# A transformer block on one core: the planner's order replaced by a fixed list, weights split into more tiles, other early loads

## The chip, the cores and the metric

One core of one Trainium2 chip runs the whole kernel. The metric is the device time in microseconds (us) of one execution; lower is better. The core's engines work from queues of their own: PE (TensorE, matmuls; its weight loads are shown as PEld), DVE (VectorE), ACT (ScalarE), POOL (GpSimd) and SP (SyncE, which here issues all transfers but one). They wait for one another by semaphores only.

## What is computed

One transformer block over 2048 rows of 512 columns, in bf16: conditioned layernorm, attention over eight earlier positions in steps of two, and a gated feed-forward layer.

```python
mod = (silu(c) @ w_mod).reshape(1, 6, 1, 512)
sa, ca, ga, sb, cb, gb = mod[:, 0], mod[:, 1], mod[:, 2], mod[:, 3], mod[:, 4], mod[:, 5]
h = layernorm(x) * (1 + ca) + sa
x = x + ga * A(h, wqkv, wo)
h = layernorm(x) * (1 + cb) + sb
x = x + gb * ((gelu(h @ w_gate) * (h @ w_up)) @ w_down)
...
# A: 32 heads of 16; q, k, v = h @ wqkv; position s sees s, s-2, ... s-14
logits = einsum('bhsd,bhswd->bhsw', q, kg) * 16 ** -0.5
o = einsum('bhsw,bhswd->bhsd', softmax(logits), vg)
return o.reshape(B, S, D) @ wo
```

## The kernel before

**Tiling.** The rows are split into five groups of 256, 256, 512, 512 and 512 (`GROUPS`, line 198); group 0 is the first. Everything but x is held with the columns on the partitions. For each group the kernel emits these steps:
- `ln` (line 419): statistics on DVE (L442, L444), the inverse root on POOL (L448), the normed rows xn on DVE (L452), their transpose (on PE, L476, for the first norm of groups 0 to 2 and the second of group 0; otherwise by a transposing DMA, L459), and the scaling by the modulation (ACT L490 or L464, for group 0 also DVE L485), which gives hT or, for the second norm, h2T.
- `emit_qkv` (line 498): the projections (L527), 12 tiles of a PSUM bank for a group of 512 rows, 6 for one of 256, each of 16 or 8 matmuls, copied out by ACT (L532) to qT, kT and vT. vT goes to DRAM (`scr`, L537) and comes back as four shifted loads (`vR`, L541).
- `emit_attention` (line 551): products of q and shifted k on DVE (`pq`, 1.16 us each in a row), folded over the head's 16 columns by PE (L585), a softmax (maxima on DVE L607 to L611, their subtraction on PE L616, exponentials on ACT L623, sums on PE L635, reciprocals on DVE L639, their broadcast on PE L647), products with v (`pv`), folded by PE (L678), the output projection (L693), and the residual sum on DVE (L697); then the second norm.
- `emit_ffn` (line 703): 14 blocks of 128 gate and up columns (L716; two blocks to a tile for 256 rows), gelu on ACT, the product on DVE, and the down matmuls (L738) in chunks of four, four, four and two; then the residual sum (`ot`, L745) and the store.
The gates ga and gb are multiplied into wo (`woP`, L760) and w_down (`WdP`, L763, seven pieces) by DVE.

**What orders the work.** Nothing is issued where it is written. `pe`, `act`, `dve`, `gp` and `dma` append an operation with a cost, its operands, and a priority to a list; `Plan.order` (line 88) then simulates the engines and always takes the operation that can start soonest, by priority among equals. Its transfers cost bytes over a bandwidth (360 GB/s unless given), one behind the other on a queue, and land 2.0 us later. `emit` (line 152) issues the operations in that order, and each engine, and SP with its transfers, runs its part of it strictly in order. The tile framework adds the semaphores, by the tiles and ranges of tiles that instructions touch.

**Loads.** SP first issues x's rows 0 to 255, two blocks of w_mod (512 columns each, for sa and ca), the three parts of wqkv (v, q, k) into one tile, then the rest of the first 1024 rows of x and the other early weights (lines 337 to 351). `late_loads` (line 353) holds gate, up, down and the later x back until group 0's vR has been issued. Warm-up matmuls (L366) run from 1.3 to 6.0 us, and `keep_warm` (L373) repeats two of them at two places, to have PE busy ahead of the first projection.

Of the kernel before, what the change touches and what calls it, by code (L numbers as in the profile page):

```python
# [15 lines left out]
NEG = -1.0e9  # L16

# [22 lines left out]
class Plan:  # L40
# [3 lines left out]
    AHEAD = 3.0  # L44
    MARGIN = {"pe": 0.3, "act": -0.2, "dve": -0.2, "pool": 0.0, "sp": 0.0}
# [42 lines left out]
    def order(self):  # L88
        for o in self.ops:
            for p in o.pre | o.after:  # L90
                p.post.append(o)
        n_pre = {o: len(o.pre | o.after) for o in self.ops}
        ready = [o for o in self.ops if not n_pre[o]]
        engines, pipe, table = {}, {}, None
        placed, made = [], {t: [] for t in self.tags}
        seen = set()

        def start(o):
            at = max([p.end - (p.lat if p.eng == o.eng and not p.dma else 0.0) for p in o.pre], default=0.0)
            for t in o.tiles:  # L100
                if t.tag is not None and t not in seen:
                    before = self.seqs[t.seq][t.at - 1] if t.at else None
                    if before is not None and before not in seen and before not in o.tiles:
                        return None
                    got, bufs = made[t.tag], self.tags[t.tag][1]
                    if len(got) >= bufs:
                        if got[-bufs].left:
                            return None
                        at = max(at, got[-bufs].free)
            return at  # L110

        while ready:
            best = None
            for o in ready:
                at = start(o)
                if at is None:
                    continue
                free = engines.get(o.eng, 0.8)
                if o.dma:
                    at = max(at, pipe.get(o.eng, 0.0) - self.AHEAD)  # L120
                key = (max(free, at + self.MARGIN[o.eng]), o.pri)
                if best is None or key < best[0]:
                    best = (key, o, max(free, at))
            if best is None:
                raise RuntimeError("no operation can be placed: " + str([(o.eng, o.pri) for o in ready]))
            _, o, at = best
            ready.remove(o)
# [35 lines left out]
class Engines:  # L163
    def __init__(self, nc, pl):
        op = pl.op
# [4 lines left out]
        self.dma = lambda n, fn, bw=360e3, **kw: op("sp", 0.55, fn, dma=n / bw, **kw)  # L170
# [3 lines left out]
def kernel(  # L174
# [31 lines left out]
    for tag, bufs in (("xs", 4), ("wqkv", 1), ("woP", 1), ("Wg", 1), ("Wu", 1), ("WdP", 1), ("st", 3), ("mv", 4),  # L206
# [25 lines left out]
    PRI_QKV = (-60, 30, 50, 130, 1050)  # L232

# [27 lines left out]
    def consts_pool():  # L261

# [5 lines left out]

        nc.gpsimd.memset(BC[:], 0.0)
# [9 lines left out]

# [12 lines left out]
    gp(5.0, consts_pool, r=[ident], w=[M, F1, NB, BC, MA, MB], pri=-900)  # L292
# [3 lines left out]
    wqkv = T("wqkv", [P, DT, 3 * D], BF16, "wqkv")  # L296
    woP = T("woP", [P, 4, D], BF16, "woP")
    Wg = T("Wg", [P, DT, F], BF16, "Wg")
    Wu = T("Wu", [P, DT, F], BF16, "Wu")
    WdP = T("WdP", [P, FT, D], BF16, "WdP")  # L300
    wm = [T({2: "oT"}.get(b, "h2T"), [P, 4, D], BF16, "wm") for b in range(6)]
# [14 lines left out]
    def load_x(lo, hi, p, after=()):  # L316
        dma(131e3 * (hi - lo), lambda: nc.sync.dma_start(
# [4 lines left out]
    def load_wm(b, p, after=()):  # L322
        dma(524e3, lambda: nc.sync.dma_start(
# [3 lines left out]
    def load_wqkv(b, p):  # L327
        dma(524e3, lambda: nc.sync.dma_start(
            out=wqkv[:, :, b * D:(b + 1) * D],
            in_=A_wqkv[:, b * D:(b + 1) * D].rearrange("(dt p) n -> p dt n", p=P)), w=[(wqkv, b)], pri=p)  # L330

    act(0.1, lambda: nc.scalar.dma_start(out=crow[:], in_=c), w=[crow], pri=-1000, lat=3.0)
    def load_w(t, src, p, after):
        dma(1835e3, lambda: nc.sync.dma_start(out=t[:], in_=src.rearrange("(dt p) f -> p dt f", p=P)), w=[t], pri=p,
            after=after)

    load_x(0, 2, -1000)
    load_wm(0, -999)
    load_wm(1, -998)
    for i, b in enumerate((2, 0, 1)):  # L340
        load_wqkv(b, -997 + i)
    load_x(2, 4, -990)
    load_x(4, 8, -989)
    load_wm(2, -988)
    for d4 in range(4):
        dma(131e3, lambda d4=d4: nc.sync.dma_start(
# [5 lines left out]

    def late_loads(after):
        load_w(Wg, B_w_gate, -894, after)
        load_w(Wu, B_w_up, -893, after)
        load_x(8, 12, -892, after)
        load_wm(5, -891, after)
        load_w(WdP, B_w_down, -890, after)
        load_x(12, 16, -889, after)
# [24 lines left out]
    pe(0.3, c_cols, r=[crow, one1], w=[c_ps], pri=-990)  # L384
    act(0.2, lambda: nc.scalar.activation(out=scT[:], in_=c_ps[:], func=ACT.Silu), r=[c_ps], w=[scT], pri=-990,
# [3 lines left out]
    def mod_cols(b, b2, p, off):  # L389
        mps = T("psF", [P, 8], F32, "modT_ps")  # L390

        def cols(bb, half):
            for ch in range(4):
                col = half * 4 + ch
                for kt in range(4):
                    nc.tensor.matmul(mps[:, col:col + 1], lhsT=wm[bb][:, kt, ch * P:(ch + 1) * P],
                                     rhs=scT[:, kt:kt + 1], start=(kt == 0), stop=(kt == 3))

        pe(0.42, lambda: cols(b, 0), r=[wm[b], scT], w=[(mps, 0)], pri=p)
        if off == 0:  # L400
            keep_warm(2, (mps, 0), p)
        pe(0.42, lambda: cols(b2, 1), r=[wm[b2], scT], w=[(mps, 1)], pri=p)
# [16 lines left out]
    def ln(g, dst, off, p, seq, tags=("psF", "psF"), sums=None):  # L419
# [49 lines left out]
        for dtp in range(2):  # L469
# [10 lines left out]
            if p == -960 and dtp == 1:  # L480
                keep_warm(2, tp, p)
            for dd in range(2):
                dt = 2 * dtp + dd
                if p == -960 and dd == 1:
                    dve(0.35, lambda dt=dt, dd=dd, tp=tp: nc.vector.tensor_scalar(  # L485
                        out=dst[:, 0:n // P, dt, :], in0=tp[:, dd, 0:n].rearrange("p (c s) -> p c s", s=P), scalar1=scl[:, off // 2 + dt:off // 2 + dt + 1],
# [4 lines left out]
                    out=dst[:, 0:n // P, dt, :], in_=tp[:, dd, 0:n].rearrange("p (c s) -> p c s", s=P), func=ACT.Identity,  # L491
# [307 lines left out]
```

## Time and profile before

| | |
|---|---|
| time, median of 3 runs | 260.44 us (259.02 to 260.95) |
| span of the profiled execution, first to last instruction | 260.6 us |
| PE busy | 242.4 us (93%) |
| DVE busy | 165.3 us (63%) |
| ACT busy | 156.6 us (60%) |
| moved by DMA | 28.84 MB |

The profile is of one execution, and its span is its own time to within what the runs differ by. Busy times of PE are modelled from a pipeline: a matmul is shown with 0.38 us (512 columns) and in a row one starts every 0.216, so the spacing counts and not the mean. The granted clock of PE is given as a share of full speed: 1.00 is 2.4 GHz, 0.50 is 1.2 GHz. "Idle before" in brackets is the time an engine stood still ahead of an instruction, with what ended it.

### The profile page before, as it was taken

What the parts mean: (1) busy time and instruction counts of PE and PEld (TensorE: products, weight loads), DVE (VectorE), ACT (ScalarE), POOL (GpSimd) and SP (SyncE); (2) the same over time, 40 slices, a digit from 0 to 9 for tenths busy, and PEclk for the clock granted to TensorE, in tenths of its full rate; (3) what the DMA queues carried; (4) which work ended last, traced back from release to release, by engine and by line L of the source; (5) the groups of instructions that cost most, each with busy time, mean ns of one, the idle gap of its engine ahead of it and who ended that gap; (6) DMA issues with size and microseconds to landing.
All of it is one profiled execution on the core that took longest, in us unless ns stands there. A gap on an engine that the chain in (4) does not pass through costs nothing.

```text
span 260.6 us, 4271 instructions
## 1 busy us (share of the span) xinstructions
PE 242.4 (93%) x1617; PEld 126.8 (49%) x1632; DVE 165.3 (63%) x313; ACT 156.6 (60%) x278; POOL 21.9 (8%) x43
## 2 busy tenths in 40 slices
PE   7399979979996999999999999999999999999993
PEld 2277735448742477446544444344344444444441
DVE  3277578899999479986289988349946222222111
ACT  2127767676666789748967748943758730666400
POOL 8010200210022000002000005000002000000000
PEclk9869979979999999999999999999999999999999
DMA  6997999999902566405912502210002201100011
GB/s 203 353 252 192 273 399 351 282 233 207 149 3 40 121 160 167 88 3 144 185 43 58 105 3 40 40 43 20 21 0 44 40 0 43 40 0 0 0 43 40
DMA packets 36550, 28.84 MB, mean 111 GB/s; under 512 B 12849, under 2 KB 34610, under 8 KB 36530
## 3 DMA queue, kind: packets, MB, share of 16 engines
q1 hardware_dynamic: 36528, 28.56, 44.6%
q8 instruction: 13, 0.21, 0.4%
q14 instruction: 7, 0.06, 0.1%
q10 hardware_dynamic: 2, 0.00, 0.0%
HBM read 21.40 MB, written 4.28 MB: 99 GB/s over the span
## 4 chain that ended last, share of the span: by engine, by line
PE 83%; DVE 6%; DMA 4%; ACT 3%; issue 1%; POOL 1%; SPq 1%; DVEq 0%; POOLq 0%; ACTq 0%
PE u_ps L716 19%; PE g_ps L716 19%; PE y_ps L738 17%; PE qkv_ps L527 16%; PE x_ps L693 5%; DMA wqkv<-in_A_wqkv_dram 4%; PE o_ps L678 3%; PE LT L585 2%; DVE pq L569 2%; POOL rstd L448 1%; ACT hT L490 1%; DVE st L442 1%; DVE xn L452 1%; PE LT L616 1%; PE rB L647 1%
## 5 line engine op out<-in xcount | busy, mean ns | idle before, releaser
L716 PE MATMUL u_ps<-h2T,Wu 128*128 128x512 bf16 (+1 forms) x280 | 58.5, 341 | 0.0
L716 PE MATMUL g_ps<-h2T,Wg 128*128 128x512 bf16 (+1 forms) x280 | 58.4, 340 | 0.0
L738 PE MATMUL y_ps<-WdP,hht 128*128 128x512 bf16 x216 | 50.3, 379 | 3.0 <-DVE WdP L763 2.5
L527 PE MATMUL qkv_ps<-hT,wqkv 128*128 128x512 bf16 (+1 forms) x240 | 48.7, 358 | 3.7 <-DMA wqkv<-in_A_wqkv_dram 3.2
L725 ACT ACTIVATE gl<-g_ps 128x512 bf16<-128x512 f32 x56 | 33.6, 599 | 29.3 <-PE g_ps L716 29.1
L727 ACT CAST ub<-u_ps 128x512 bf16<-128x512 f32 x56 | 32.8, 586 | 19.8 <-PE u_ps L716 19.8
L728 DVE TENSOR_TENSOR hht<-gl,ub 128x512 bf16<-128x512 bf16 x56 | 23.6, 423 | 32.1 <-ACT ub L727 31.7
L716 PEld LDWEIGHTS <-Wg 128*128 128x128 bf16 x280 | 27.3, 99 | 22.8 <-issue 1.7
L716 PEld LDWEIGHTS <-Wu 128*128 128x128 bf16 x280 | 27.3, 99 | 22.4 <-issue 1.3
L527 PEld LDWEIGHTS <-wqkv 128*128 128x128 bf16 x240 | 27.2, 118 | 22.7 <-issue 8.7
L738 PEld LDWEIGHTS <-hht 128*128 128x128 bf16 x224 | 21.3, 98 | 29.1 <-issue 4.6
L448 POOL TENSOR_TENSOR rstd<-rstd,neghalf 128x2 f32<-128x2 f32 x16 | 16.9, 1077 | 177.0 <-DVE xsum L431 102.5
L569 DVE TENSOR_TENSOR pq<-qT,kT 128x2048 bf16<-128x2048 bf16 x24 | 28.6, 1218 | 0.0
L662 DVE TENSOR_TENSOR pv<-e,vR 128x2048 bf16<-128x2048 bf16 x24 | 28.4, 1219 | 0.0
L745 DVE TENSOR_TENSOR ot<-y_ps,x_sg 128x512 bf16<-128x512 f32 x16 | 10.5, 685 | 23.1 <-PE y_ps L738 23.1
L693 PE MATMUL x_ps<-woP,oT 128*128 128x512 bf16 x59 | 14.9, 379 | 0.3
L434 ACT ACTIVATE xn<-x_sg,xsum 128x512 bf16<-128x512 bf16 x16 | 11.4, 714 | 4.8 <-DVE xsum L431 4.8
L532 ACT CAST kT<-qkv_ps 128x512 bf16<-128x512 f32 x16 | 9.4, 588 | 7.7 <-PE qkv_ps L527 6.5
L532 ACT CAST qT<-qkv_ps 128x512 bf16<-128x512 f32 x16 | 9.4, 586 | 7.3 <-PE qkv_ps L527 7.3
L442 DVE BATCH_NORM_STATS2 st<-x_sg 128x6 f32<-128x512 bf16 x16 | 10.2, 682 | 5.3 <-DMA x_sg<-in_A_x_dram 5.3
L532 ACT CAST vT<-qkv_ps 128x512 bf16<-128x512 f32 x16 | 9.2, 588 | 7.1 <-PE qkv_ps L527 6.7
L697 DVE SCALAR_TENSOR_TENSOR x_sg<-x_ps,x_sg 128x512 bf16<-128x512 f32 x16 | 10.8, 688 | 3.3 <-PE x_ps L693 3.3
(86 smaller groups left out, 189.5 us busy)
## 6 DMA issues: line engine op xcount, KB each, us to landing
vR<-scr SPq DMA_DIRECT2D x24, 260.0 KB, 5.5
wm<-in_w_mod_dram SPq DMA_DIRECT2D x6, 512.0 KB, 7.1
vR<-scr SPq DMA_DIRECT2D x8, 264.0 KB, 5.7
out_dram<-ot SPq DMA_DIRECT2D x16, 128.0 KB, 1.7
Wg<-in_B_w_gate_dram SPq DMA_DIRECT2D x1, 1792.0 KB, 11.2
Wu<-in_B_w_up_dram SPq DMA_DIRECT2D x1, 1792.0 KB, 15.1
WdP<-in_B_w_down_dram SPq DMA_DIRECT2D x1, 1792.0 KB, 12.9
scr<-vT SPq DMA_DIRECT2D x6, 264.0 KB, 2.6
```

The lines of the kernel that those rows point to most:

```text
L442: dve(0.62, lambda i=i, st=st, c0=c0: nc.vector.bn_stats(out=st[:, i, :], in_=x[g, c0 + i]), r=[x.key(g, c0 + i)], w=[(st, i)], pri=p)
L448: gp(0.7, lambda rstd=rstd: nc.gpsimd.tensor_tensor(out=rstd[:], in0=rstd[:], in1=neghalf[:, 0:2], op=ALU.pow), r=[rstd, neghalf], w=[rstd ...
L527: nc.tensor.matmul(ps[:, j - j0, :], lhsT=wqkv[:, dt, b * D + j:(b + 1) * D:4], rhs=hT[g][:, 0:n // P, dt, :], start=(dt == 0), stop=(dt = ...
L532: act(0.49, lambda t=t, off=off, j0=j0, ps=ps: nc.scalar.copy(out=t[:, j0:j0 + nj, off:off + n], in_=ps[:]), r=[ps], w=[(t, j) for j in ra ...
L569: dve(1.16, lambda j=j, wg=wg, t=pq[m]: nc.vector.tensor_tensor(out=t[:], in0=_ap(q[g][:, j, 0:n], [[0, 4], [1, n]]), in1=_ap(k[g][:, j, : ...
L662: dve(1.16, lambda jj=jj, jl=jl, wg=wg, t=pv[m]: nc.vector.tensor_tensor(out=t[:], in0=_ap(e[:, wg, :], [[0, 4], [1, n]]), in1=vR[g][jj][: ...
L693: nc.tensor.matmul(x1_ps[:], lhsT=oT[:, j, c4 * P:(c4 + 1) * P], rhs=woP[:, j, :], start=(j == 0), stop=(j == 3))
L716: nc.tensor.matmul(ps[:, ft - f0, :], lhsT=Wt[:, dt, ft * P:(ft + 1) * P], rhs=h2[g][:, 0:n // P, dt, :], start=(dt == 0), stop=(dt == DT ...
L725: act(0.5, lambda gl=gl, ps=gu[0]: nc.scalar.activation(out=gl[:], in_=ps[:], func=ACT.Gelu_apprx_tanh), r=[gu[0]], w=[gl], pri=p, table=" ...
L727: act(0.49, lambda ub=ub, ps=gu[1]: nc.scalar.copy(out=ub[:], in_=ps[:]), r=[gu[1]], w=[ub], pri=p)
L728: dve(0.37, lambda gl=gl, ub=ub, ht=ht: nc.vector.tensor_tensor(out=ht[:], in0=gl[:], in1=ub[:], op=ALU.mult), r=[gl, ub], w=[ht], pri=p)
L738: nc.tensor.matmul(y_ps[:], lhsT=hh[ft // nf][:, ft % nf, c4 * P:(c4 + 1) * P], rhs=WdP[:, ft, :], start=(ft == 0), stop=(ft == FT - 1))
```

## The change

**The order.** `Plan.order` no longer chooses. A list `ORDER` of 951 operation numbers (in the order in which the program appends them) gives the order; `order` only walks it and computes each operation's planned start `at`, with all transfers on one pipe and a ninth transfer waiting for the landing of the one eight before it. The list puts the parts of a group freely: tiles of one projection or gate and up blocks come in any sequence, and those of different groups are mixed. Decoded, PE's order begins: warm-up, column matmuls of c, fill, modulation 0 and 1, group 0's transposes and fills, group 1's transposes, group 0's projections (q, q, k, v, v, k), group 2's transposes and group 1's projections mixed, group 0's first fold and mask, and from there 12 tiles of group 2's and 10 of group 3's projections between the steps of the first two softmaxes, group 0's and 1's folds and modulation 5, 2, 3, 4, until the first gate tile of group 0 (G0). Group 4's projections stand among group 0's gate and up. At the end PE has three output tiles of group 4 mixed and then all 14 matmuls of the fourth. DVE takes group 3's statistics after group 0's four pq, group 4's in part ahead of group 0's reciprocal, and five of WdP's scalings ahead of group 3's maxima. SP's order begins:

```
x 0-255, x 256-511, x 512-1023, wm01, wq, wkv, woP[3], x 1024-1535, woP[2], woP[1],
x 1536-2047, wm5, scr(0), wm2, vR(0) three pieces, transpose of group 3 (first half), vR(0) fourth piece,
wm3, transpose of group 3 (second half), woP[0], scr(1), Wu[1], vR(1) one piece, Wg[1], wm4, vR(1) two pieces,
scr(2), vR(1) fourth piece, Wg[0], Wu[0], transpose of group 4, ...
```

**Tiles and loads.** wqkv becomes two tiles, wq and wkv (one load each); Wg and Wu become two halves each of 896 columns; the first two blocks of w_mod come as one load wm01 of 1024 columns, into the buffer that WdP takes later; WdP is loaded in two halves. `late_loads` is gone: only the list holds these loads back.

**Layout.** hT and h2T of the groups transposed on PE are `[P, DT, SG]`, so that each of the four column blocks is contiguous; before, all were `[P, 4, DT, P]`.

**Fills.** `keep_warm` becomes `fill`: an operation of planned cost 0.02 whose number of matmuls is set after ordering from the planned gap to PE's next operation. There are four, and group 0's first projection is kept behind them all. The constants of POOL become three operations instead of one.

```diff
+ORDER = [
+    0, 6, 39, 40, 41, 28, 9, 131, 132, 1, 4, 133, 134, 135, 42, 43, 11, 7, 5, 29, 30, 31, 3, 253, 33, 35, 38, 254, 44,
...
+]
...
+        placed = [self.ops[i] for i in ORDER]
...
+            if o.dma and len(landed) >= self.LANES:
+                at = max(at, landed[-self.LANES])
...
+                pipe = max(pipe, at + us) + o.dma
+                o.end = pipe + 2.0 + o.late
...
     def emit(self):
         placed = self.order()
+        pes = [o for o in placed if o.eng == "pe"]
+        for o, q in zip(pes, pes[1:]):
+            if hasattr(o, "fill"):
+                o.fill = max(0, int((q.at - o.at - 0.25) / 0.216))
...
-    wqkv = T("wqkv", [P, DT, 3 * D], BF16, "wqkv")
+    wq = T("wqkv", [P, DT, D], BF16, "wq")
+    wkv = T("wkv", [P, DT, 2 * D], BF16, "wkv")
...
+    Wg = [T("Wg", [P, DT, F // 2], BF16, "Wg") for _ in range(2)]
+    Wu = [T("Wu", [P, DT, F // 2], BF16, "Wu") for _ in range(2)]
+    wm01 = T("WdP", [P, 4, 2 * D], BF16, "wm01")
...
+    def load_cols(t, src, lo, hi, p, bw=380e3):
+        dma(1024.0 * (hi - lo), lambda dq: dq.dma_start(
+            out=t[:], in_=src[:, lo:hi].rearrange("(t p) n -> p t n", p=P)), w=[t], pri=p, bw=bw)
...
     load_x(0, 2, -1000)
-    load_wm(0, -999)
-    load_wm(1, -998)
-    for i, b in enumerate((2, 0, 1)):
-        load_wqkv(b, -997 + i)
-    load_x(2, 4, -990)
+    load_cols(wm01, w_mod, 0, 2 * D, -999)
+    load_cols(wq, A_wqkv, 0, D, -998)
+    load_x(2, 4, -997)
+    load_cols(wkv, A_wqkv, D, 3 * D, -996)
...
-    def late_loads(after):
-        load_w(Wg, B_w_gate, -894, after)
...
+    for i in range(2):
+        load_cols(Wg[i], B_w_gate, i * F // 2, (i + 1) * F // 2, -894 + 2 * i)
+        load_cols(Wu[i], B_w_up, i * F // 2, (i + 1) * F // 2, -893 + 2 * i)
...
-    def keep_warm(n, after, p):
+    fills = []
+
+    def fill(after):
         def run():
-            for i in range(n):
+            for i in range(o.fill):
                 nc.tensor.matmul(wps[:], lhsT=warm[:, 0:P], rhs=warm[:], start=True, stop=True)
...
+        o = pe(0.02, run, r=[warm, after], w=[wps], pri=-960)
+        o.fill = 0
+        fills.append(o)
...
-                        out=dst[:, 0:n // P, dt, :], in0=tp[:, dd, 0:n].rearrange("p (c s) -> p c s", s=P), scalar1=scl[:, off // 2 + dt:off // 2 + dt + 1],
+                        out=dst[:, dt, 0:n], in0=tp[:, dd, 0:n], scalar1=scl[:, off // 2 + dt:off // 2 + dt + 1],
```

## Rows read from the trace of the kernel before

**Rows 1.** The page: busy time of the engines, and the granted clock in 40 slices
```profile
PE 242.4 (93%) x1617; PEld 126.8 (49%) x1632; DVE 165.3 (63%) x313; ACT 156.6 (60%) x278; POOL 21.9 (8%) x43
...
PEclk9869979979999999999999999999999999999999
```

**Rows 2.** Windows by stage: length, busy us of each engine (instructions), PEclk, DMA share, GB/s
```profile
13.50:94.00 80.50, 72.96 (x626) 46.32 (x631) 65.17 (x133) 53.37 (x96) 8.68 (x9) 0.93 0.84 204
...
94.00:256.20 162.20, 161.68 (x934) 77.03 (x941) 94.97 (x166) 100.55 (x177) 7.57 (x6) 1.00 0.23 52
```

**Rows 3.** The chain that ended last, in order of time: start us, us, what
```profile
3.47 9.93 DMA wqkv<-in_A_wqkv_dram
...
13.53 7.61 PE qkv_ps L527 x48
...
21.75 1.84 ACT hT L490 x4
...
26.96 0.99 PE LT L585 x32
...
34.95 7.73 PE qkv_ps L527 x28
...
60.88 0.87 PE g_ps L716 x8
...
132.92 0.86 PE g_ps L716 x4
```

**Rows 4.** Windows over PE's gaps and the slow stretches, columns as in rows 2
```profile
10.40:13.50 3.10, 0.00 (x0) 0.00 (x0) 0.41 (x1) 0.84 (x2) 0.00 (x0) 0.63 1.09 347
...
17.00:18.00 1.00, 1.00 (x7) 0.67 (x6) 1.00 (x3) 0.58 (x1) 0.00 (x0) 0.50 1.08 232
...
32.00:34.80 2.80, 0.82 (x19) 0.62 (x18) 0.98 (x3) 2.79 (x5) 0.00 (x0) 1.00 1.03 401
...
53.00:55.10 2.10, 0.32 (x2) 0.09 (x1) 2.00 (x9) 1.84 (x4) 0.03 (x1) 1.00 1.10 270
...
57.00:58.00 1.00, 1.00 (x6) 0.73 (x5) 0.97 (x3) 0.74 (x2) 0.00 (x0) 0.50 1.10 225
...
81.40:83.90 2.50, 0.01 (x2) 0.03 (x1) 2.50 (x11) 2.50 (x6) 0.59 (x1) 1.00 0.00 0
```

**Rows 5.** Timeline, first and last scaling of group 0's input: start us, us, what
```profile
9.78 0.41 DVE L485 TENSOR_SCALAR hT<-tp,scl,modT 128x256 bf16<-128x256 bf16 x1 [2.02 <-ACT scl L403]
...
11.28 0.41 DVE L485 TENSOR_SCALAR hT<-tp,scl,modT 128x256 bf16<-128x256 bf16 x1 [1.09 <-ACT hT L490]
```

**Rows 6.** The wqkv loads' issue and landing times, and two PE steps of the modulation
```profile
2.37 1.85 SPq L328 DMA_DIRECT2D wqkv<-in_A_wqkv_dram  x3
...
DMA to landing us min/median/max: 8.0/9.0/9.9
...
5.92 0.25 PE L382 MATMUL c_ps<-one,crow 1*128 1x1 bf16 x4
...
8.92 0.55 PE L396 MATMUL modT_ps<-scT,wm 128*128 128x1 bf16 x16 [0.55 <-DMA wm<-in_w_mod_dram]
```

**Rows 7.** Windows: rates of the transfers, in the last column
```profile
0.00:5.00 5.00, 3.74 (x11) 1.42 (x12) 1.53 (x5) 1.28 (x1) 3.92 (x21) 1.00 0.55 179
...
5.00:10.00 5.00, 3.34 (x52) 2.04 (x51) 1.77 (x8) 0.41 (x3) 1.70 (x8) 1.00 1.01 334
...
10.00:15.00 5.00, 1.82 (x10) 1.04 (x9) 1.43 (x4) 1.02 (x2) 0.00 (x0) 0.62 1.11 340
...
50.00:60.00 10.00, 7.77 (x87) 4.89 (x85) 9.65 (x29) 7.29 (x15) 2.54 (x3) 0.83 1.15 221
```

**Rows 8.** Window from the first attention product to group 0's second norm
```profile
20.90:52.50 31.60, 28.54 (x286) 17.66 (x285) 25.23 (x52) 21.64 (x41) 4.01 (x5) 0.95 1.04 300
```

**Rows 9.** The page, DMA issues: KB each, median us to landing
```profile
vR<-scr SPq DMA_DIRECT2D x24, 260.0 KB, 5.5
```

**Rows 10.** Timeline, the last two output additions
```profile
256.13 1.29 DVE L745 TENSOR_TENSOR ot<-y_ps,x_sg 128x512 bf16<-128x512 f32 x2 [4.75 <-PE y_ps L738]
```

More of the change, by code (lines that the diff above doesn't have):

```diff
@@ L40 @@
 class Plan:
[L44 to L45 removed]
+    LANES = 8
     def __init__(self, tc):
@@ L88, in order @@
     def order(self):
[L89 to L99, printed above, removed]
+        engines, pipe, table, landed = {}, 0.0, None, []
+        made, seen = {t: [] for t in self.tags}, set()
+        placed = [self.ops[i] for i in ORDER]
+        assert sorted(ORDER) == list(range(len(self.ops)))
+        for o in placed:
+            at = engines.get(o.eng, 0.8)
+            for p in o.pre:
+                at = max(at, p.end - (p.lat if p.eng == o.eng and not p.dma else 0.0))
             for t in o.tiles:
                 if t.tag is not None and t not in seen:
-                    before = self.seqs[t.seq][t.at - 1] if t.at else None
-                    if before is not None and before not in seen and before not in o.tiles:
-                        return None
+                    seen.add(t)
                     got, bufs = made[t.tag], self.tags[t.tag][1]
                     if len(got) >= bufs:
-                        if got[-bufs].left:
-                            return None
+                        assert not got[-bufs].left
                         at = max(at, got[-bufs].free)
[L110 to L127, printed above, removed]
+                    got.append(t)
             us = o.us
@@ L204, in pool @@
         pl.tag(tag, ctx.enter_context(tc.tile_pool(name=tag, bufs=bufs, **kw)), bufs)
-    for tag, bufs in (("xs", 4), ("wqkv", 1), ("woP", 1), ("Wg", 1), ("Wu", 1), ("WdP", 1), ("st", 3), ("mv", 4),
+    for tag, bufs in (("xs", 4), ("wqkv", 1), ("wkv", 1), ("woP", 1), ("Wg", 2), ("Wu", 2), ("WdP", 1), ("st", 3), ("mv", 4),
                       ("rstd", 4), ("xsum", 4), ("xn1", 2), ("xn2", 2), ("hT", 2), ("qT", 2), ("kT", 2), ("vT", 2), ("vR", 3), ("prod", 6),
@@ L392, in cols @@
         def cols(bb, half):
+            src, at = (wm01, bb * D) if bb < 2 else (wm[bb], 0)
             for ch in range(4):
@@ L518, in emit_qkv @@
         if g == 0:
-            order = [(b, j) for b in (2, 0, 1) for j in range(0, 4, nj)]
+            order = [(b, j) for b in range(3) for j in range(0, 4, nj)]
         for step, (b, j0) in enumerate(order):
@@ L526, in mm @@
                     for dt in range(DT):
-                        nc.tensor.matmul(ps[:, j - j0, :], lhsT=wqkv[:, dt, b * D + j:(b + 1) * D:4],
-                                         rhs=hT[g][:, 0:n // P, dt, :], start=(dt == 0), stop=(dt == DT - 1))
-            pe(0.866, mm, r=[(wqkv, b), hT[g]], w=[ps], pri=p)
+                        nc.tensor.matmul(ps[:, j - j0, :], lhsT=(wkv[:, dt, (b - 1) * D + j:b * D:4] if b else wq[:, dt, j:D:4]), rhs=h_cols(hT, g, dt), start=(dt == 0), stop=(dt == DT - 1))
+            pe(0.866, mm, r=[wkv if b else wq, hT[g]], w=[ps], pri=p,
+               after=fills if g == 0 and step == 0 else ())
             t, off = (q, k, v)[b][g], (0, HALO, HALO)[b]
@@ L536, in emit_qkv @@
             scr = T("scr", [P, njv, row], BF16, "scr")
-            dma(P * njv * row * 2, lambda i=i, scr=scr: nc.sync.dma_start(
+            dma(P * njv * row * 2, lambda dq, i=i, scr=scr: dq.dma_start(
                 out=scr[:], in_=v[g][:, njv * i:njv * (i + 1), 0:row]),
```

104 lines of the change are left out of this document (49 added, 55 removed), and 40 rows, old and new, of the table ORDER.

## The prediction

> **What bounds the kernel now.** I read the page first: TensorE (PE) is busy 93% of the 260.6 us span, and in the slices of 6.5 us its granted clock falls below 0.9 only in slices 2, 3, 6 and 9 [rows 1]. The windows by stage say where the other 7% lies. From 94.0 to 256.2 us PE is busy 161.7 of 162.2 us at full clock. From 13.5 us, where the first projection (the q, k, v matmuls) begins, to 94 it is busy 73.0 of 80.5 us at a mean clock of 0.93 [rows 2]. So an order of the work can win nothing behind 94 us and some 13 us before it.
>
> Then I listed what PE loses between 13.5 and 94 us, from the chain of work that ended last and from windows laid over the gaps [rows 3, 4].
> - Half clock at the start: 48 projection matmuls of 256 columns take 7.61 us. Eight of that size take 0.87 us at full clock, so 48 should take 5.2: 2.4 lost. The granted clock was still 0.50 at 17 to 18 us; from 10.4 to 13.5 PE had stood empty.
> - 32.0 to 34.8 us: busy 0.82 of 2.80, in the first softmax: 2.0 lost. Then half clock again: 28 records of 512 columns take 7.73 us, where 28 x 0.216 (0.86 for four) is 6.05: 1.7 lost.
> - 53.0 to 55.1: busy 0.32 of 2.10, the second softmax and the norm before the first gate matmul: 1.8 lost, and half clock behind it (0.50 at 57 to 58).
> - 81.4 to 83.9: 2.5 lost, DVE busy without a break.
> All idle time is 80.5 - 73.0 = 7.5; less 2.0, 1.8 and 2.5 it leaves 1.2 of small waits, among them group 1's projections, which wait for four scaled inputs one after the other (ACT hT, 1.84 us). The mean clock of 0.93 means 5.6 us; less 2.4 and 1.7 it leaves 1.5 for the third dip. Sum 7.5 + 5.6 = 13.1. At the tail two output additions run one behind the other after the last matmul, 1.29 us [rows 10].
>
> **The change part by part.** *Early loads.* Before the first projection stand, now, 0.26 MB of x, 1.05 of w_mod and 1.57 of wqkv. The three wqkv pieces are issued from 2.37 to 4.2 us and land 8.0, 9.0 and 9.9 us later, the first at 10.4 and the last at 13.4; PE starts at 13.5, after the last, though its first tile needs only the v piece, issued first [rows 3, 6]. Three loads in one tile make that wait, and tiles of their own end it. But the new queue sends x's first 1.05 MB ahead of w_mod. By the rates [rows 7] 0.90 MB had moved by 5 us and 2.57 by 10. The second w_mod block (1.31 MB down the queue) let PE go on at 8.92 [rows 6], when 2.2 MB had moved, and the last wqkv piece (2.88 MB) came when 3.7 had: a load lands when 0.86 MB more than the bytes up to it have moved. So wm01 (2.10 MB) lands at 2.96 MB: 11.2 us at 340 GB/s, 10.2 at the 401 GB/s of the wide weight loads [rows 4]. I take 11.0, near the early rows since x and wq keep narrow rows: the modulation is whole 2 us later than now. wq (2.62 MB) comes at 12.4 (11.5 to 12.7), wkv (3.67) at 15.3 (14.1 to 15.8). Behind wm01 stand two groups of 16 matmuls (1.1), two small copies (0.3) and the four scalings of hT, now in single file between DVE and ACT from 9.78 to 11.69 [rows 5]; with each column block contiguous I take 1.2, two beside two (1.0 to 1.9). First projection: 13.6 us (12.5 to 14.5). No gain: the freed wait is eaten by the later w_mod. The first k tile has to wait for wkv only if both q tiles are done by 15.3; at half clock (1.7 us each) they are not.
>
> *Fill matmuls.* They cost nothing where they fit, as PE has no other work there; one too many delays the next step by 0.2 us. Their number is the planned gap over 0.216. The first gap, behind the column matmuls of c that end at 6.2 [rows 6], reaches to wm01. The plan's own terms (bytes over 360 or 380 GB/s, plus 2.0) set that at 9.0, hence about 9 fills, to 8.1 us. By the rows wm01 is at 11.0: PE empty for 2.9 us. Gaps of 3.1, 2.0 and 1.8 us were followed by half clock, one of 2.5 was not [rows 4]. I keep the first loss of 2.4 us.
>
> *Order of the middle.* Projections of groups 2 and 3 now stand inside the first two softmaxes. Before the first gate matmul PE has 96 x 0.109 + 88 x 0.216 of projections (29.5), three folds of 0.99 [rows 3], 16 matmuls of 512 columns for output projection and modulation (3.5), and 4.7 of transposes, one-column matmuls and softmax steps as the timeline has them: 40.7 us. From 13.6, with 2.4 for the clock, that ends at 56.7. DVE must be ready by then. Its first product needs two q tiles and a k tile, 18.6 at half clock, and a cast of 0.6: 19.2 (17.0 at full clock). From there to the input of group 0's second norm the trace has 25.2 us of DVE work [rows 8]; the new order puts in group 4's statistics (3.1), group 3's norms (1.5), the second softmax's maxima (0.9) and one norm more (0.4), and takes out group 2's (2.1): 29. That is 48.2, with 2 us of waits 50.2, the norm with POOL's root 1.9, transposes and four scalings on ACT 3: 55.1. PE comes 1.6 us later, so the gaps of 2.0, 1.8 and 1.2 go, with the half clock behind them (3.2). The gap of 2.5 goes too: five of WdP's seven scalings stand ahead of group 3's maxima, the other two right behind, and the first down matmul after those. What is late next is the softmax itself: at the first output fold, the second maxima and the second sums PE arrives 0.5 to 1 us before DVE or ACT by this count, and so again in group 2. I take 4 us for all of them (0 to 8; nearest are the two old softmax gaps, 3.8).
>
> *SP queue.* A transfer that waits holds up all behind it. Group 3's two transposing DMAs stand ahead of vR0's last piece and of woP's last quarter, and wait for norms that DVE makes at about 28 and 34 us. Behind them are 5.9 MB (scr and vR of group 1, the gate and up halves), issued from about 35. Stretches full of vR move 221 GB/s [rows 7], and a piece takes 5.5 us to land [rows 9]. 1.05 MB of vR at 200, a little below that, and 4.87 at 375, between the 347 and 401 of rows 4, take 18.2 us, the landing 2.4 (0.86 MB at some 350): the second half needed, Wu0, lands at 55.6 and is wanted at 57.6. Cost nothing; the cover is 2 us. vR0's last piece lands at 35.3 where DVE wants it at 34.5: 0.8, inside the 4.
>
> *Tail.* The last 14 matmuls belong to one output tile: one addition behind them, 0.6 us less.
>
> Sum: gone 7.5 idle, 1.7 and 1.5 of half clock, 0.6 of tail = 11.3; come 4.0 of waits and 0.1 of start; kept 2.4 of half clock. 260.6 - 11.3 + 4.1 = 253.4. The profiled span is 0.2 above the median of the three runs: 253, rounded.
>
> **Rivals.** *The fills hold the clock.* If wm01 lands at the 10.2 of the wide rate, PE never stands empty for more than 2.1 us; then the 2.4 go as well, and 0.8 of the start: 249.8. For it: 401 GB/s in the wide loads [rows 4]. Against it: 334 to 340 GB/s in these very microseconds [rows 7]. The Trainium skill ("DMA: Bandwidth & Descriptors", section "Measured (HBM→SBUF, 128 partitions, SWDGE, issued from GpSimd)") asks for transfers of 1 MiB and more, for three quarters of the peak; it measured another queue than SP's, and wm01 and wkv become such transfers here. By its 425 GB/s for very large ones wm01 would, as an estimate, land a little before 10. No row of this trace reaches that rate in the first 15 us.
>
> *Moved, not removed.* DVE is the bound of the first 70 us: it was busy 25.2 of 31.6 us with all its waits [rows 8], and 2.0 of 2.1 and 2.5 of 2.5 in two of PE's gaps [rows 4]. If each hand-over costs more than I count, PE waits 8 us instead of 4 and falls to half clock once more (1.7): 258.8, no change that can be told. Against it: the chain has PE work beside each softmax step.
>
> *The weights come late (slower).* Place: the gate and up halves at the end of the SP queue's first part, behind transposes and vR. If those 5.9 MB move at vR's 200 GB/s and not at the mixture's 325, they need 29.6 us, Wu0 lands at 67 and PE stands from 57.6 on: 9.4, and half clock behind it 1.7: 264.1. It decides slower from a landing at 66 us on, and takes half of the gain from 61. Against it: 401 GB/s while Wg and Wu move now [rows 4], with vR just ahead of them.
>
> **How the numbers follow.** The forecast 0.64 (249 to 257), the held clock 0.14, moved 0.15, late weights 0.07. A measurement of this kernel can tell about 1%, 2.6 us, from no change. Faster by more: the first two, 0.78. Within: 0.15. Slower: 0.07. Low end of the range: no loss of clock and half the waits, 247.5 with the early start; high end the second rival, 259.
>
> **What would show it.** Right: the first projection at 13 to 14 us and half clock behind it to about 18; then PE without half clock, its waits 4 us in all up to 94, and the first gate matmul at 55 to 58. Wrong: an empty PE of more than 2 us behind 20 us; a gate or up matmul that waits for a DMA; a first projection before 12.5, or at full clock.

## The result, and the profile after

The changed kernel takes 253.05 us (median of 4, 250.94 to 259.33; the highest ran at a lower clock and is left out of the ratio, and without it the median is 252.75); the kernel before, in the runs beside it, 260.69 (259.02 to 261.98). The ratio is 0.967 [0.960, 0.975]: faster. The profiled execution has a span of 250.5 us.

The page of the changed kernel, as [rows 1]: busy time by engine, and the granted clock in 40 slices.

```profile
PE 240.7 (96%) x1637; PEld 126.4 (50%) x1637; DVE 165.9 (66%) x313; ACT 153.4 (61%) x278; POOL 17.9 (7%) x43
...
PEclk9859999999999999999999999999999999999999
```

PE is busy for about as long as before (240.7 us, before 242.4). Of the four slices with a low clock only the second and the third (6.3 to 18.8 us) are left. The windows by stage, as [rows 2]: start and end, length, then busy us of PE, PEld, DVE, ACT, POOL, then PE's clock, DMA share and GB/s.

```profile
13.50:94.00 80.50, 77.94 (x701) 49.88 (x700) 71.85 (x131) 65.21 (x120) 6.12 (x10) 0.97 0.90 216
...
20.00:94.00 74.00, 71.89 (x663) 44.94 (x662) 67.23 (x119) 61.38 (x112) 4.64 (x6) 1.00 0.89 211
...
94.00:247.00 153.00, 153.00 (x864) 71.27 (x861) 86.18 (x160) 85.09 (x153) 5.24 (x6) 1.00 0.21 49
```

From 13.5 to 94 us PE is busy 77.9 us where it was 73.0, and the clock is 0.97 where it was 0.93. Behind 20 us there is no half clock left (1.00), and PE stands still for 2.1 us (74.00 - 71.89). DVE and ACT do more of their work here (71.9 and 65.2 us, before 65.2 and 53.4): 35 attention products on DVE where there were 24, and 47 copies of projections on ACT where there were 35. That work ran behind 94 us before. Behind 94 us PE was almost without a gap before (161.7 of 162.2 us, [rows 2]) and is without one now.

The start, in PE's timeline (start us, us, what; in brackets the idle time before it and what ended it):

```profile
5.94 2.12 PE L403 MATMUL warm_ps<-warm 128*128 128x512 bf16 x9
...
10.59 0.99 PE L429 MATMUL modT_ps<-scT,wm 128*128 128x1 bf16 x32 [2.53 <-DMA wm<-in_w_mod_dram]
...
13.10 0.42 PE L562 MATMUL qkv_ps<-hT,wq 128*128 128x256 bf16 x1
...
13.97 3.36 PE L562 MATMUL qkv_ps<-hT,wq 128*128 128x256 bf16 x15 [0.45 <-DVE hT L520]
```

Nine fills run to 8.06, then PE stands empty for 2.5 us until wm01 is in. The two modulation blocks are whole 2 us later than before (the second then began at 8.92, [rows 6]). The first q tile waits once more, for a scaling of hT. Then 15 matmuls take 3.36 us, twice the 1.64 that they take at full clock (0.109 us each, as the prediction has it). Three windows over this stretch, columns as above:

```profile
9.00:10.00 1.00, 0.00 (x0) 0.00 (x0) 1.00 (x4) 0.00 (x0) 0.00 (x0) 1.00 1.08 389
...
14.00:15.00 1.00, 1.00 (x6) 0.70 (x6) 1.00 (x4) 0.98 (x3) 0.00 (x0) 0.50 1.10 327
...
18.00:19.00 1.00, 1.00 (x12) 1.00 (x10) 0.00 (x0) 0.50 (x1) 0.00 (x0) 1.00 1.16 347
```

The clock was still 1.00 at 9 to 10 us, when PE did nothing; it is 0.50 at 14 to 15, with PE at work, and full again by 18 to 19. What PE waits for in the whole span (total us, times, longest us), the lines of the stretch before 94 us:

```profile
PE modT_ps L429 <- DMA wm<-in_w_mod_dram: 2.5, 1, 2.5
...
PE u_ps L749 <- DMA Wu<-in_B_w_up_dram: 1.3, 1, 1.3
...
PE o_ps L711 <- DVE pv L701: 0.6, 1, 0.6
...
PE qkv_ps L562 <- DVE hT L520: 0.4, 1, 0.4
```

The softmax waits that I had put first are not among the larger ones. One that I had priced at nothing is there: the first wait for an up weight, 1.3 us. That place in PE's timeline:

```profile
55.55 1.05 PE L749 MATMUL g_ps<-h2T,Wg 128*128 128x256 bf16 x8
...
57.87 2.79 PE L749 MATMUL u_ps<-h2T,Wu 128*128 128x256 bf16 x24 [1.27 <-DMA Wu<-in_B_w_up_dram]
```

DVE at the start, and its one addition at the end, as [rows 5] and [rows 10]:

```profile
13.19 0.73 DVE L520 TENSOR_SCALAR hT<-tp,scl,modT 128x256 bf16<-128x256 bf16 x2 [2.21 <-ACT hT L525]
...
19.12 2.36 DVE L608 TENSOR_TENSOR pq<-qT,kT 128x2048 bf16<-128x2048 bf16 x2 [1.55 <-ACT kT L567]
```

```profile
247.14 0.69 DVE L778 TENSOR_TENSOR ot<-y_ps,x_sg 128x512 bf16<-128x512 f32 x1 [1.92 <-PE y_ps L771]
```

The first attention product starts at 19.12; the last output tile has one addition behind it instead of two.

### The profile page after: what moved, and what is told of

The parts are those of the page before. It is cut to its first block, busy times and chain, and to the rows that moved or that the text cites. A ratio compares the mean times of both kernels' runs of the same rounds, so it can differ in the third digit from the quotient of the medians.

```text
span 250.5 us, 4243 instructions
## 1 busy us (share of the span) xinstructions
PE 240.7 (96%) x1637; PEld 126.4 (50%) x1637; DVE 165.9 (66%) x313; ACT 153.4 (61%) x278; POOL 17.9 (7%) x43
## 4 chain that ended last, share of the span: by engine, by line
PE 81%; DMA 10%; SPq 3%; ACT 2%; DVE 2%; issue 1%; DVEq 0%; ACTq 0%
PE u_ps L749 19%; PE y_ps L771 19%; PE g_ps L749 19%; PE qkv_ps L562 10%; PE x_ps L726 5%; DMA Wu<-in_B_w_up_dram 5%; DMA wm<-in_w_mod_dram 3%; PE o_ps L711 3%; PE LT L618 3%; DMA vR<-scr 2%; DVE pv L701 2%; SPq L358 1%; SPq L576 1%; PE LT L649 1%; SPq L347 1%
## 5 line engine op out<-in xcount | busy, mean ns | idle before, releaser
L749 PE MATMUL u_ps<-h2T,Wu 128*128 128x512 bf16 (+1 forms) x280 | 55.1, 337 | 1.3 <-DMA Wu<-in_B_w_up_dram 1.3
L749 PE MATMUL g_ps<-h2T,Wg 128*128 128x512 bf16 (+1 forms) x280 | 55.4, 337 | 0.0
L562 PE MATMUL qkv_ps<-hT,wkv 128*128 128x512 bf16 (+1 forms) x160 | 31.8, 340 | 0.0
L483 POOL TENSOR_TENSOR rstd<-rstd,neghalf 128x2 f32<-128x2 f32 x16 | 12.7, 803 | 179.6 <-DVE rstd L472 157.8
L562 PEld LDWEIGHTS <-wkv 128*128 128x128 bf16 x160 | 17.2, 115 | 9.1 <-issue 1.5
L562 PE MATMUL qkv_ps<-hT,wq 128*128 128x512 bf16 (+1 forms) x80 | 18.1, 367 | 0.7 <-DVE hT L520 0.4
L499 ACT ACTIVATE h2T<-h2T,modT,scl 128x512 bf16<-128x512 bf16 (+1 forms) x16 | 11.1, 756 | 9.5 <-DMA h2T<-xn 9.5
L726 PE MATMUL x_ps<-woP,oT 128*128 128x512 bf16 x64 | 16.1, 379 | 0.0
L717 ACT CAST oT<-o_ps 128x512 bf16<-128x512 f32 x16 | 8.7, 594 | 8.0 <-PE o_ps L711 8.0
L562 PEld LDWEIGHTS <-wq 128*128 128x128 bf16 x80 | 9.2, 121 | 5.8 <-issue 1.3
```

The source lines that it names most:

```text
L483: gp(0.7, lambda rstd=rstd: nc.gpsimd.tensor_tensor(out=rstd[:], in0=rstd[:], in1=neghalf[:, 0:2], op=ALU.pow), r=[rstd, neghalf], w=[rstd ...
L499: act(0.2 + n * 0.001, lambda dt=dt: nc.scalar.activation(out=dst[:, 0:n // P, dt, :], in_=dst[:, 0:n // P, dt, :], func=ACT.Identity, sca ...
L562: nc.tensor.matmul(ps[:, j - j0, :], lhsT=(wkv[:, dt, (b - 1) * D + j:b * D:4] if b else wq[:, dt, j:D:4]), rhs=h_cols(hT, g, dt), start=( ...
L726: nc.tensor.matmul(x1_ps[:], lhsT=oT[:, j, c4 * P:(c4 + 1) * P], rhs=woP[:, j, :], start=(j == 0), stop=(j == 3))
L749: nc.tensor.matmul(ps[:, ft - f0, :], lhsT=Wt[ft // 7][:, dt, ft % 7 * P:(ft % 7 + 1) * P], rhs=h_cols(h2, g, dt), start=(dt == 0), stop=( ...
```

## The experiments

All were timed beside the kernel before, whose medians in these batches are 261.7 to 262.2 us. "Changed kernel" is the one of the diff; a ratio is always to the kernel before.

**Where the gain comes from: tiles or list.** First, the kernel before with wqkv in three tiles and nothing else.

```diff
-    wqkv = T("wqkv", [P, DT, 3 * D], BF16, "wqkv")
+    wqkv = [T("wqkv", [P, DT, D], BF16, "wqkv") for _ in range(3)]
...
-            out=wqkv[:, :, b * D:(b + 1) * D],
+            out=wqkv[b][:],
```

> The kernel before with wqkv in three tiles, one load each, and nothing else changed. If the first projection of the kernel before waited for all three pieces only because they are one tile, it now starts at 11.8 us (v piece landed at 10.4, scaled input ready at 11.7) instead of 13.5, PE stands empty for 1.4 us instead of 3.1, and the half clock behind it (2.4 us) may go too: span 1.7 to 4 us below the kernel before if PE's time is the bound from there, less if DVE or ACT set the later steps. Rival: the wait is one of the transfers themselves (the v piece isn't there earlier): start 13.5, span unchanged.

Measured: 261.11 us (median of 10), ratio 0.994 [0.989, 0.998]. The first projection in PE's timeline, and the stretch from 20 to 94 us in the windows:

```profile
11.52 5.43 PE L527 MATMUL qkv_ps<-hT,wqkv 128*128 128x256 bf16 x48 [1.72 <-DMA wqkv<-in_A_wqkv_dram]
```

```profile
20.00:94.00 74.00, 67.09 (x596) 41.88 (x598) 61.12 (x124) 51.79 (x90) 7.99 (x8) 0.95 0.87 206
```

The projections start at 11.52 instead of 13.53 and run at full clock, 48 in 5.43 us instead of 7.61. That is 4 us won by 17 us: three loads in one tile made that wait, as the prediction has it. And the profiled execution, the fastest of the ten, shows it in its time (258.11 us, mean clock 0.987). One other is like it (258.47, 0.985); the other eight have mean clocks of 0.959 to 0.980 and take 260.2 to 264.8, as long as the kernel before at such clocks (260.7 at 0.979). So the split shows its gain only in the two executions that lose less clock; where the others lose it, their times don't tell. The 1.7 to 4 us that I expected came in those two alone. Behind 20 us nothing is changed: PE is idle for 6.9 us at a clock of 0.95, with the old waits (2.5 for a WdP scaling, 1.8 for a scaling of h2T, 1.0 and 0.9 in the softmax). Second, the converse: the changed kernel's tiles, loads, layout and fills under the old planner, with the late loads held back as before.

```diff
-        placed = [self.ops[i] for i in ORDER]
+        while ready:
+            best = None
+            for o in ready:
...
```

> The changed kernel's tiles, loads, layout and fills, but ordered by the planner of the kernel before, with the late loads held back as there. Theory: most of the gain is the list's, in the middle. Then this is 3 to 8 us slower than the changed kernel: 255 to 261 us as timed, with 4 us or more of empty PE and at least one spell of half clock between 20 and 94 us. Rival: tiles and early loads carry the gain: within 2 us of the changed kernel.

Measured: 269.59 us, ratio 1.028 [1.021, 1.034]: slower than before, and almost 9 us above the 255 to 261 that I expected. The same window:

```profile
20.00:94.00 74.00, 60.25 (x529) 36.42 (x532) 57.07 (x120) 44.52 (x79) 8.28 (x8) 0.88 0.81 186
```

The first projection and one later place, in the timelines of PE and DVE:

```profile
11.29 1.90 PE L592 MATMUL qkv_ps<-hT,wq 128*128 128x256 bf16 x15 [1.10 <-DVE hT L550]
...
43.83 1.29 DVE L507 BATCH_NORM_STATS2 st<-x_sg 128x6 f32<-128x512 bf16 x2 [3.25 <-DMA x_sg<-in_A_x_dram]
...
49.38 0.40 PE L651 MATMUL LT<-pq,Mph 128*32 128x256 bf16 x8 [2.20 <-DVE pq L641]
```

PE reaches the first projection earlier than in the changed kernel (15 matmuls from 11.29, at full clock; the planner sends wm01 and wq behind only 0.26 MB of x, the list behind 1.05) and then stands for 13.75 us of 74, at a clock of 0.88. On the same tiles the list, of all engines and of the transfers, is worth about 269.6 - 253.1 = 16.5 us (two batches). Tiles and list don't add up: the old order on the new tiles loses 8 us.

**One tile for wq and wkv under the list.**

```diff
-    wq = T("wqkv", [P, DT, D], BF16, "wq")
-    wkv = T("wkv", [P, DT, 2 * D], BF16, "wkv")
+    wqkv = T("wqkv", [P, DT, 3 * D], BF16, "wqkv")
...
+    load_part("q", 0, D, -998)
+    load_part("kv", D, 3 * D, -996)
```

> The changed kernel with wq and wkv as two loads into one tile. Theory of the shared tile: the first projection waits for the kv load too, so it starts at about 15.5 us instead of 13.1 (14.0 for the run of matmuls), and the span is 1.5 to 2.4 us longer. Rival: the tile makes no difference (the first projection at 13 to 14): same time within 0.5 us.

Measured: 259.37 us, ratio 0.987 [0.978, 0.995]. Expected was a loss of some 2 us against the changed kernel; it is 5 by the two ratios, 6 to 7 by the medians. What SP's queue waits for, its timeline, and PE's:

```profile
SPq L361 <- PE qkv_ps L565: 12.9, 1, 12.9
...
2.87 13.82 SPq L361 DMA_DIRECT2D wqkv<-in_A_wqkv_dram  x2
```

```profile
12.94 3.36 PE L565 MATMUL qkv_ps<-hT,wqkv 128*128 128x256 bf16 x15 [0.85 <-DVE hT L523]
...
22.09 5.12 PE L565 MATMUL qkv_ps<-hT,wqkv 128*128 128x256 bf16 x32 [5.79 <-DMA wqkv<-in_A_wqkv_dram]
```

I had looked for a wait of PE for the later load. What comes is a wait of the queue: the load of k and v, now into another part of the tile that the q matmuls read, stands still on SP for 12.9 us until they are done, is issued at 16.3 us instead of 3.4, and holds up all transfers behind it. PE waits 5.8 us for it. So the split is worth more than the wait of one projection: this list places the load of k and v behind the q matmuls, and only with tiles of their own does the load not wait for them.

**The fills.** None at all (the output does not use them), then 11 more in the first gap.

```diff
-                o.fill = max(0, int((q.at - o.at - 0.25) / 0.216))
+                o.fill = 0
```

> The changed kernel without its fill matmuls (nine of them, 5.9 to 8.1 us). They compute nothing that is used. Theory: they end 2.5 us before w_mod lands and so don't hold the clock; without them PE is empty from 6.0 to 10.6, the clock falls earlier, and it rises at the same place or a little earlier, since the same dense work brings it back: time the same within 1 us. Rival: they save part of the half clock: 1 to 2.5 us slower without them.

Measured: 253.29 us, ratio 0.966 [0.959, 0.973], as the changed kernel. PE's timeline:

```profile
9.76 0.98 PE L429 MATMUL modT_ps<-scT,wm 128*128 128x1 bf16 x32 [2.41 <-DMA wm<-in_w_mod_dram]
...
13.13 3.36 PE L562 MATMUL qkv_ps<-hT,wq 128*128 128x256 bf16 x15 [0.45 <-DVE hT L520]
```

The 15 matmuls take the same 3.36 us without any fill. The two profiles differ by less than the edit: the 14 warm-up matmuls ahead took 5.91 us here and 4.57 in the changed kernel, so that PE's empty gap is 2.41 us here and 2.53 there. That the nine fills as sized gain nothing rests on the times, not on this pair of profiles.

```diff
+                o.fill += 11 if first else 0
+                first = False
```

> The changed kernel with 20 fill matmuls in the first gap instead of 9, so that they end at about 10.4 us, when w_mod lands (9.8 to 10.6 in the traces). Theory: the empty 2.5 us ahead of w_mod cost the half clock; with them filled PE stays at full clock, the first 47 projection matmuls take 5.2 us instead of 7.1, and the span falls by 1 to 2 us. Rival: the time before 20 us is hidden by what follows (the weights of the gate and up matmuls land when they land): the wait for Wu grows from 1.3 to 3 us and the time stays within 0.7 us.

Measured: 251.35 us (250.45 to 253.84), ratio 0.963 [0.958, 0.968]. The profiled one took 253.70:

```profile
14.24 1.80 PE L564 MATMUL qkv_ps<-hT,wq 128*128 128x256 bf16 x15 [0.95 <-DVE hT L522]
...
55.15 1.05 PE L751 MATMUL g_ps<-h2T,Wg 128*128 128x256 bf16 x8 [1.29 <-DMA Wg<-in_B_w_gate_dram]
...
57.41 4.23 PE L751 MATMUL u_ps<-h2T,Wu 128*128 128x256 bf16 x24 [1.22 <-DMA Wu<-in_B_w_up_dram]
```

With 20 fills the q run is at full clock: 1.80 us instead of 3.36. But PE then comes earlier to the gate matmuls, waits 1.29 for Wg and 1.22 for Wu, and behind these two waits 24 matmuls take 4.23 us where the changed kernel's took 2.79. In this execution the gain was eaten, by the late weights. It is one of two with a mean clock of 0.993 (253.7 and 253.8 us); the four others, at 0.997 to 1.000, took 250.5 to 251.4. The 1 to 2 us that I expected are not shown against the changed kernel: the two intervals overlap.

**The weights' order on SP's queue.** The list sends Wu[1] and Wg[1] before Wg[0] and Wu[0], which are needed first. Here the four places are filled in the order of need (the numbers of the list, decoded):

```diff
-    Wu[1] ... Wg[1] ... Wg[0] ... Wu[0]
+    Wg[0] ... Wu[0] ... Wu[1] ... Wg[1]
```

> The changed kernel with the four gate and up halves loaded in the order in which PE first needs them (Wg0, Wu0, Wu1, Wg1), in the same places of the SP queue. Theory: the 1.27 us for which PE waited for Wu goes, since Wu0 is now second of the four, and nothing is late in its place (Wg1 lands near 58, wanted at 63): 1 to 1.3 us faster. Rival: the third half, Wu1, is then the late one and PE waits for it instead: no change.

Measured: 251.81 us, ratio 0.963 [0.959, 0.968]. In PE's timeline the first gate and up tiles wait for nothing:

```profile
13.00 3.07 PE L558 MATMUL qkv_ps<-hT,wq 128*128 128x256 bf16 x15 [0.95 <-DVE hT L516]
...
54.13 1.04 PE L745 MATMUL g_ps<-h2T,Wg 128*128 128x256 bf16 x8
...
55.01 2.78 PE L745 MATMUL u_ps<-h2T,Wu 128*128 128x256 bf16 x24
```

The wait of 1.27 is gone. The gates come 1.4 us earlier, but the q run, which this edit does not touch, also started 1.0 earlier in this execution. A wait of 1.3 for a softmax reciprocal is new. Alone the order gains 0.8 us on the changed kernel's median in the batch below (252.61), within what two such medians differ by: the 1 to 1.3 us that I expected are not shown.

**wm01 ahead of x's third load.** The statistics of those rows of x move back with it.

```diff
-    ... 43, 11, 7, ...
+    ... 43, 7, 11, ...
```

> The changed kernel with wm01 issued ahead of x's rows 512 to 1023 (0.52 MB less in front of it), and the statistics of those rows moved behind the first four norms on DVE. Theory: w_mod lands 1.4 us earlier (near 9.0), the first projection starts near 12.2, now held by wq (landed 12.1), and the gap ahead of w_mod shrinks from 2.5 to about 1 us, so the half clock may go as well: 1 to 3 us faster. Rival: the landing is not set by the bytes ahead: no difference in the landing, time within 0.7 us.

Measured: 253.15 us, ratio 0.968 [0.963, 0.972]: no gain.

```profile
9.41 0.95 PE L425 MATMUL modT_ps<-scT,wm 128*128 128x1 bf16 x32 [0.35 <-DMA wm<-in_w_mod_dram]
...
12.96 0.30 PE L558 MATMUL qkv_ps<-hT,wq 128*128 128x256 bf16 x1 [1.69 <-DMA wq<-in_A_wqkv_dram]
```

wm01 is in at 9.41, 1.2 us earlier, and the projection still starts at 12.96: now wq is the last to come, 1.69 us after PE is ready. The bytes ahead of wq are still 2.10 MB, 1.05 of them x. They need not be: the planner's kernel above has 1.31 MB there, and its q run began at 11.29, at full clock. Under the list that was not tried.

**The layout.** The changed kernel with hT and h2T as `[P, 4, DT, P]` again.

```diff
-    hT[g] = T("hT", [P, 4, DT, P] if LN1_TAGS[g] is None else [P, DT, SG], BF16, "hT")
+    hT[g] = T("hT", [P, 4, DT, P], BF16, "hT")
```

> The changed kernel with the column blocks of hT and h2T interleaved as in the kernel before. Theory: the scalings of group 0 run in single file between DVE and ACT again, the first projection's run of matmuls starts 0.7 to 1 us later, and group 0's second norm loses little as its four scalings are all on ACT: 0.5 to 1 us slower. Rival: no difference, the order of the two engines being set by the PSUM tile they read.

Measured: 252.41 us, ratio 0.965 [0.961, 0.968]: no difference, where I had expected 0.5 to 1 us.

```profile
10.88 1.02 PE L429 MATMUL modT_ps<-scT,wm 128*128 128x1 bf16 x32 [2.85 <-DMA wm<-in_w_mod_dram]
...
14.29 3.36 PE L562 MATMUL qkv_ps<-hT,wq 128*128 128x256 bf16 x15 [0.45 <-DVE hT L520]
```

From modulation to the q run it is 3.41 us here and 3.38 with the new layout (10.59 to 13.97).

**Both repairs, beside the changed kernel itself.** Three kernels on one chip: the changed kernel unaltered, 20 fills with the weights in order of need, and these two with wm01 first (and 14 fills, as the gap is shorter).

```diff
+                o.fill += 11 if first else 0
...
-    Wu[1] ... Wg[1] ... Wg[0] ... Wu[0]
+    Wg[0] ... Wu[0] ... Wu[1] ... Wg[1]
```

> The changed kernel itself, beside the two versions below on the same chip. 251 to 254 us as timed, ratio 0.960 to 0.972; the half clock between the first idle gap and 17 to 18 us in every execution, and a wait for Wu of 0.5 to 1.5 us.

> Both edits that each took a known loss away: 20 fills in the first gap, and the gate and up halves in the order of their first use. Alone, the longer fill won 2 us before 20 us and lost them again in a wait of 2.5 us for Wg and Wu near 55; the other order took the wait for Wu away but kept half a spell of half clock. Theory: the gains add, since the one makes room for the other: no half clock before 20 us, first gate matmul near 53, waits for its weights under 1.3 us (the third half, Wu1, is now the late one): 249 to 250.5 us as timed, 2 to 3 us below the changed kernel. Rival: something else is late by as much (Wu1, or the softmax steps on DVE): within 1 us of it.

> As the version before, but with wm01 also ahead of x's rows 512 to 1023 and seven more fills instead of eleven. Alone, that move brought w_mod to 9.4 us but PE then waited 1.7 us for wq. Theory: no more than the version before, since wq is the bound there: within 0.7 us of it. Rival: 1 us faster, as the modulation is no longer in the way.

Measured: the changed kernel 252.61 us (251.85 to 256.47), ratio 0.967 [0.961, 0.972]; both repairs 250.01 (249.05 to 251.65), 0.959 [0.954, 0.964]; with wm01 first as well 252.01, 0.966 [0.959, 0.972]. The gates in the changed kernel's profile of this batch, an execution of 256.18 us:

```profile
58.46 1.89 PE L749 MATMUL g_ps<-h2T,Wg 128*128 128x256 bf16 x8 [2.79 <-DMA Wg<-in_B_w_gate_dram]
...
60.73 3.32 PE L749 MATMUL u_ps<-h2T,Wu 128*128 128x256 bf16 x24 [0.38 <-DMA Wu<-in_B_w_up_dram]
```

The late weight is the gate's here, and the wait for Wu is below the 0.5 us that I expected. Nor is the half clock there in every execution: one of the six has a mean clock of 0.999 and yet takes 252.07 us, no less than its neighbours at 0.993 (251.85 to 252.68). The clock of the kernel with both repairs on its page, and its timeline:

```profile
PEclk9999999999999999999999999999999999999999
```

```profile
11.66 0.94 PE L427 MATMUL modT_ps<-scT,wm 128*128 128x1 bf16 x32
...
14.79 1.80 PE L560 MATMUL qkv_ps<-hT,wq 128*128 128x256 bf16 x15 [0.95 <-DVE hT L518]
...
54.34 1.04 PE L747 MATMUL g_ps<-h2T,Wg 128*128 128x256 bf16 x8
...
55.21 2.78 PE L747 MATMUL u_ps<-h2T,Wu 128*128 128x256 bf16 x24
```

No slice has a low clock (the six executions: 0.998 to 1.000), the modulation waits for nothing behind the fills, and neither gate nor up waits. All six of its times lie below all six of the changed kernel beside it: 2.6 us by the medians, 2.3 without its two executions at 256. So it is faster than the changed kernel and the kernel before. Each repair alone had 0.963 in another batch; that the two add up is not shown, as the intervals overlap. With wm01 first PE waits 1.2 us for wq again, and 2.0 us of the gain are gone, where I had expected to stay within 0.7.

## Why the prediction was right, and where it was not

The forecast was 253.0 and the time is 253.05, but the sum behind it was 2.9 us too high and the step from span to time about as much too low. Term by term from the first projection's run of matmuls, each for the profiled execution in us (PE's work is what the other terms leave of the span):

| term | predicted | measured |
|---|---|---|
| start of the first projection's run | 13.6 | 13.97 |
| lost to half clock there | 2.4 | 2.0 |
| PE's waits behind it, to 94 | 4.0 | 2.1 |
| PE's work without gaps (the rest) | 229.6 | 229.0 |
| from the last matmul to the end | 3.8 | 3.4 |
| span | 253.4 | 250.5 |

- **The mechanism** held: the order wins only before 94 us, by filling the softmax gaps with projections, and the half clock behind those gaps goes with them. The old order on the new tiles loses just there. What the list's order of PE's work gives and what its order of transfers gives was not tried apart.
- **The signs named beforehand.** Those of being right came (first projection at 13.1, half clock to about 18 and none behind, first gate matmul at 55.55), but for the waits, 2.1 us instead of 4. One of those of being wrong came too: an up matmul waits for a DMA (1.27).
- **Landing of the early loads.** The step "a load lands when 0.86 MB more than the bytes up to it have moved" gave 11.0, 12.4 and 15.3 us; wm01 let PE go on at 10.59, and wq and wkv landed at 12.07 and 15.5. "No gain: the freed wait is eaten by the later w_mod" is borne out for this queue: the start is 13.1 and the run 13.97, before 13.53. But w_mod alone is not the cause: with wm01 first, wq takes its place, and ahead of both stands x. The Trainium skill's figure for very large transfers ("DMA: Bandwidth & Descriptors", "Measured (HBM→SBUF, 128 partitions, SWDGE, issued from GpSimd)") would, as an estimate, have had wm01 in before 10; in the profiled execution the trace does not agree (10.59).
- **Fills and half clock.** 9 fills to 8.1 us and an empty PE of 2.9: 9 fills to 8.06, empty for 2.5. The lost 2.4 was 2.0 (47 matmuls took 7.11 us; at 0.109 each, 5.1). That this loss is the empty gap's was argued from [rows 4]; it is shown by the profiles of the two kernels with 20 fills, where the q run is at full clock though 0.95 us of waiting for a scaling is left ahead of it. The rival "the fills hold the clock" was wrong in that these fills do it. Its 249.8 us was not reached by longer fills alone (251.35), only nearly with the weights in order of need as well (250.01).
- **The four scalings** were taken at "1.2, two beside two". DVE stood still for 2.2 us until ACT had made its two, and the whole took 1.8 (12.13 to 13.92): still in file. The layout run shows that the contiguous columns change nothing. These 0.6 us are most of the 0.8 by which the stretch from wm01 to the q run came out longer (3.4 instead of 2.6); as wm01 came 0.4 early, the run starts 0.4 late.
- **The waits, taken at 4.0: the term that was mis-sized.** They are 2.1, and hardly the ones listed. No wait at the second maxima or the second sums came. The wait at the first output fold did, 0.6 us, but behind it stands not DVE's work: DVE waited 1.3 us for a piece of vR (0.8 named). Wu[0] cost 1.27.
- **"Cost nothing; the cover is 2 us"** for Wu[0] failed. It was put at 55.6 and wanted at 57.6; it landed at 57.8, and PE wanted it at 56.6, since the first gate tile came at 55.55 and not at 56.7. Both sides of the cover moved by 1 to 2 us. Wg[0] had no cover left either: it landed at 55.5, as PE came to it. The slower rival, late weights, thus has the right place at a seventh of its price here (1.3 of 9.4), and at more in other executions: 2.5 us with 20 fills, 3.2 in the profile beside the repairs. With the weights in order of need the wait is gone.
- **Tail.** "0.6 us less" was 1.0.
- **Span and time.** "The profiled span is 0.2 above the median" took the span for a time, as did the remark on the profile under "Time and profile before". Each execution's time stands above its span: 252.75 over 250.5 and 250.94 over 248.7 for the changed kernel, 262.06 over 260.3 and 263.54 over 261.8 before. The span of 260.6 thus belongs to an execution of about 262.3 us, 1.9 above the median of the three, and a span of 253.4 would have been a time of 255 to 256. The saved span is 10.1 us, the saved time by medians 7.6. These two errors cancel: that the forecast was so exact is luck; its sign, its place and its rough size are not.

What stays open is why the old order does so badly on the new tiles (the largest waits are for scalings of h2T and exponentials, 3.4 and 3.0 us). One link can be read in its trace: DVE stands 3.25 us until rows of x land at 43.83, which that planner had sent behind the gate and up weights, and at 49.38 PE waits 2.2 us for DVE's product. In the changed kernel all loads of x are issued by 9.3 us, and DVE waits for none of them behind that. So part of the list's worth may be its order of transfers; how much was not tried.

## What to carry to other kernels

A better order pays only where the bound engine stands still, so measure its idle time and low clock stage by stage before valuing a schedule, and price each part of a change in its new surroundings: the split alone gave 0.6%, on the old order the new tiles cost 2.8%, together they gave 3.3%. When a stage is made faster, look at what it will ask for next: in the profile with the longer fill the gain went into a wait for late weights, and the kernel was clearly faster only with the weights also put in the order in which they are needed. And take the execution's time, not its span, as the base of a sum.

## What was not expected of the hardware

- The clock's loss does not follow from a gap's length alone. Behind 2.5 us of empty PE came half clock (0.50, changed kernel); behind 2.5 us at 81.4 in the kernel before it did not [rows 4].
- One program's executions are not alike at the start. wm01 let PE go on at 9.76 to 11.03 us in four traces of kernels that send the same loads in the same order (10.59 and 11.03 for the changed kernel itself). The 14 warm-up matmuls took 4.55 to 4.83 us in five traces and 5.2 to 6.15 in the eight others; it is the same code in all, and the granted clock reads 1.00 there in either kind (changed kernel 4.57 us, split alone 6.15).
- Not of the hardware but of the semaphores that the tile framework sets: a tile shared by two loads can stop a queue and not only the reader. SP stood for 12.9 us until PE had read another part of that tile.
